# A recurrent attention and two MLPs: dummy products in one group per slot, the second MLP's weight conversion ordered behind the last attention unit

## The chip, the cores and the metric

The kernel runs on one core of one Trainium2 chip. The metric is the device time of one execution in microseconds; the kernel before takes 1383.0 us, the median of three runs (1380.85 to 1384.84).

## The reference

Three stages follow each other, all in float32 results. The first is a recurrent attention over 4 batches, 8 heads, 768 steps and a head size of 40; a 40x40 state per batch and head is read, decayed and updated at each step. Its output, 3072 tokens of 320 numbers, goes through an MLP with SiLU (320 to 2048 to 320) and then through a gated MLP (320 to 1536 twice, sigmoid gate, back to 320).

```python
for t in range(S):
    y[:, :, t] = np.einsum('bhd,bhde->bhe', rt, state)
    Sa = np.einsum('bhde,bhe->bhd', state, at)
    state = state * wt[:, :, None, :] - np.einsum('bhd,bhe->bhde', Sa, bt)
    state = state + np.einsum('bhd,bhe->bhde', vt, kt)
...
h = x @ w_in;  x = (h * sigmoid(h)) @ w_out              # first MLP
out = (sigmoid(x @ w_gate) * (x @ w_val)) @ w_out2       # second MLP
```

## The kernel before

The sequence is cut into 24 chunks of 32 steps; a chunk of one batch is a unit, so there are 96 units. One pass of the main loop (a slot) does one unit, n, on TensorE, ScalarE and VectorE in an order that is written out by hand as a string of letters: u (c_u, ps_u), R (c_rhs of the next unit, ps_r), q (c_pu, ps_lp), z and s (z_fix, ps_z, in every second slot), t (c_st, ps_t), p (prep, wt: ScalarE copies it to ks and yl), v (c_ut, ps_ut), y (c_y, ps_y: VectorE writes stg), s (c_s, ps_s, the new state). The state of unit n is wanted four units later. The digits 0 to 3 in the string are the places of the first MLP: m1_up (hp, L632) at 0 and 1, m1_down (acc, L654 to L656) at 2 and 3. The MLP lags the attention by sixteen slots, so there is none in the first sixteen; there mlp() issues dummy products instead, warm(4, 2): four products of the identity with two copies of itself (L481, acc_w), whose result nobody reads. All four products of a call go to one PSUM tile, which the next call takes anew. An opening burst of 56 such products stands ahead of the first slot.

Beside the slots run: the work on the decays of later chunks (e_work on VectorE and GpSimd, e_sys on TensorE, lb), the inversion of small triangular systems (inv_steps, on VectorE, zh and ztmp), and the conversion of the first MLP's weights. The weights come as 64-bit floats; conv_load brings a piece to a cvr tile (four of them), and conv_do makes a float32 cvt tile out of it with two ScalarE operations (L694, L695), two VectorE operations (L696, L697) and a GpSimd addition (L698). Then the piece is split into a high part (ScalarE) and a rest (VectorE).

The order of instructions on each engine is made by a scheduler with its own model of time, held by the orders that the code asks for: issue_after(x) puts what is issued in its block behind x on x's engine, without a wait between engines. in_turn() ties TensorE's work to the last product issued (last_op); behind() ties ScalarE's work behind the last unit's copy from wt (last_q["a"], L470) and VectorE's work behind the last unit's product from ps_y (last_q["v"], L575).

The second MLP's weights are converted by conv2 (L985 to L989) from the same cvr and cvt buffers, 48 pieces in all, into wgv and o tiles. Those tiles take the place of attention's in SBUF, so the last step of a piece (L988, L989) can't run before the attention is done; its first steps can. All DMAs of the kernel are issued by SP, in one queue. The second MLP then runs over 6 blocks of tokens with 12 steps of m2_up (hg, hv, L1091) and m2_down (a, L1110 to L1112).

Of the kernel before, what the change touches and what calls it, by code (L numbers as in the profile page):

```python
# [8 lines left out]
F32 = mybir.dt.float32  # L9
# [4 lines left out]
ALU = mybir.AluOpType  # L14
# [22 lines left out]
def kernel(  # L37
    ctx, tc, ins, wkab, rv, vn, w_in, w_out, w_gate, w_val, w_out2, out
):
    nc = tc.nc  # L40
# [145 lines left out]
    CW = 320  # L186
# [120 lines left out]
    def in_turn():  # L307
        return tc.issue_after(last_op[0].ins) if now[0] >= 0 else nullcontext()
# [81 lines left out]
    def behind():  # L390

        g = ExitStack()
        for x in last_q.values():
            g.enter_context(tc.issue_after(x.ins))
        return g
# [79 lines left out]
    def warm(n, w=1):  # L475

        if not n:
            return
        ps = pa.tile([128, DM], F32, tag="acc0", name="acc_w")
        for _ in range(n):  # L480
            last_op[0] = nc.tensor.matmul(  # L481
                ps[:, :128 * w], identr,
                identr.unsqueeze(1).to_broadcast([128, w, 128]), start=True, stop=True,
            )
# [139 lines left out]
    def m1_up(m, half):  # L624
        kb, p = divmod(m, NP1)
        X = X_t[kb]
        if half == 0:
            hp_t[m] = pu.tile([128, 2, 256], F32, tag="hp", name="hp")
        hp = hp_t[m]
        f = 2 * p + half  # L630
        for pi, (xi, wi_, rows) in enumerate(PASS1):
            last_op[0] = nc.tensor.matmul(  # L632
                hp[:, half, :], w1[0:rows, wi_, f * 128:(f + 1) * 128],
                X[xi][0:rows], start=(pi == 0), stop=(pi == 7),
            )
        if half == 1:
            hp_t.pop(m)
            gh = mp.tile([128, 2, 256], F32R, tag="gh", name="gh")
            gl = mp.tile([128, 2, 256], F32R, tag="gl", name="gl")

            nc.scalar.activation(hp, hp, AF.Silu, scale=wsc)  # L641
            nc.scalar.copy(gh, hp)  # L642
            nc.vector.tensor_tensor(gl, hp, gh.bitcast(F32), op=ALU.subtract)  # L643
            g_t[m] = (gh, gl)

    def m1_down(m, c):
        kb, p = divmod(m, NP1)
        gh, gl = g_t.pop(m) if c else g_t[m]
        if p == 0:
            acc_t[c] = pa.tile([128, DM], F32, tag=f"acc{c}", name=f"acc{c}")  # L650
        for fi in range(2):
            f = 2 * p + fi
            a = gh[:, fi, 128 * c:128 * c + 128]
            nc.tensor.matmul(acc_t[c], a, o1(0, f), start=(f == 0), stop=False)  # L654
            nc.tensor.matmul(acc_t[c], a, o1(1, f), start=False, stop=False)  # L655
            last_op[0] = nc.tensor.matmul(  # L656
                acc_t[c], gl[:, fi, 128 * c:128 * c + 128], o1(0, f), start=False, stop=(f == NF1 - 1)
            )
        if p == NP1 - 1:
            if c == 0:  # L660
                x2_t[kb] = mp.tile([128, 2, DM], F32, tag="cvhl", name="x2", bufs=1)
            x2 = x2_t[kb]
            nc.scalar.mul(x2[:, c], acc_t[c], wsc)  # L663
            if c:
                defer(1, lambda: nc.sync.dma_start(x2s[kb].rearrange("c p e -> p c e"), x2))
# [6 lines left out]
    def conv_load(rows, n, src, mp, cw):  # L672
        if wide:
            raw = mp.tile([128, cw, 2], I32, tag="cvr", name="cvr", bufs=4)
            t = raw.rearrange("p a b -> p (a b)")[:, :2 * n]
        else:
            raw = mp.tile([128, cw], F32, tag="cvt", name="cvt", bufs=2 + 1)
            t = raw[:, :n]
        r0 = 0
        for x in src if isinstance(src, tuple) else (src,):  # L680
            nc.sync.dma_start(t[r0:r0 + x.shape[0]], x)
            r0 += x.shape[0]
        return raw

    def conv_do(raw, rows, n, mp, cw):

        if not wide:
            return raw[:rows, :n]
        t = mp.tile([128, cw], F32, tag="cvt", name="cvt")[:rows, :n]
        lo, hi = raw[:rows, :n, 0], raw[:rows, :n, 1]  # L690
        ti = t.bitcast(I32)


        nc.scalar.mul(t, hi.bitcast(F32), 2.0 ** -112)  # L694
        nc.scalar.activation(lo, lo.bitcast(U32), AF.Copy, bias=2.0 ** 23, scale=2.0 ** -29)  # L695
        nc.vector.tensor_scalar(ti, ti, 3, None, op0=ALU.logical_shift_left)  # L696
        nc.vector.scalar_tensor_tensor(ti, hi, -0x80000000, ti, op0=ALU.bitwise_and, op1=ALU.bitwise_or)  # L697
        nc.gpsimd.tensor_tensor(ti, ti, lo, op=ALU.add)  # L698
        return t
# [85 lines left out]
    def hi_run(f, a):  # L785
        with behind(), tc.high_priority(offset=300):
            f(*a)
# [59 lines left out]
    if True:  # L847
# [12 lines left out]
        for x, t in enumerate(when):  # L860
# [7 lines left out]
            if stream[x] == e_units(gi)[-1]:  # L868
                i0 = t + 2
                i1 = min(gi * 8 - 4, i0 + 7)  # L870
                hi = lambda f: lambda *a: hi_run(f, a)
# [21 lines left out]

        def mlp(n, which):
            m = (n - 8 - 8)
            if m < 0:
                with in_turn():
                    warm(4, 2)
            if NP1 < 8 and m % 8 >= NP1:
                return  # L900
            if m < 0:
                return
            kb, p = divmod(m, 8)
            if kb >= NJ:
                return
            mm = kb * NP1 + p

            with tc.issue_after((last_op[0] if 1 else rhs_i[max(0, min(n, NS - 1) - [0, 0, 0, 0][which])]).ins):
                if which in (0, 1):
                    m1_up(mm, which)  # L910
                elif mm > 0:
                    m1_down(mm - 1, which - 2)

        for n in range(NS + 8 + 8):
# [8 lines left out]
            for o in ['cuRqz0tp1vys23l', 'zcq01uv23tpRysl'][n >= NL]:  # L923
                if o in '0123':
                    mlp(n, int(o))
# [58 lines left out]

    def conv2(tmp, src, n, hi, lo):  # L985

        w = conv_do(conv_load(128, n, src, tmp, CW), 128, n, tmp, CW)
        nc.scalar.copy(hi, w)  # L988
        nc.vector.tensor_tensor(lo, w[:lo.shape[0]], hi[:lo.shape[0]].bitcast(F32), op=ALU.subtract)  # L989

    def w2_conv(pool, tmp, x):
        f0, f1 = fc[x], min(fc[x] + 512, FF2)
        for mi in range(2):
            t = wgv[mi][x] = pool.tile([128, 6, f1 - f0], F32R, name=f"wgv{mi}_{x}")

            nc.gpsimd.memset(t[64:128, 5].bitcast(F32), 0.0)
        for o in range(f0, f1, CW2):
            n = min(CW2, f1 - o)
            c = slice(o - f0, o - f0 + n)
            for mi, w in enumerate((w_gate, w_val)):  # L1000
                t = wgv[mi][x]
                for ti in range(2):
                    conv2(tmp, wsrc(w, 128 * ti, 128, o, n), n, t[:, 2 * ti, c], t[:, 2 * ti + 1, c])

                conv2(tmp, (wsrc(w, 256, 64, o, n),) * 2, n, t[:, 4, c], t[0:64, 5, c])
# [26 lines left out]
    def o2_conv(pool, tmp, f0, f1):  # L1032
        if f1 > f0:
            t = [pool.tile([128, f1 - f0, DM], F32R, name=f"o2{y}_{f0}") for y in range(2)]
            for f in range(f0, f1):
                conv2(tmp, wsrc(w_out2, f * 128, 128, 0, DM), DM, t[0][:, f - f0], t[1][:, f - f0])
                for y in range(2):
                    o2[y].append(t[y][:, f - f0])
# [285 lines left out]
```

## Time and profile before

| | kernel before |
|---|---|
| median of three runs | 1383.0 us (1380.85 to 1384.84) |
| profiled execution, its time | 1393.2 us |
| profiled execution, its span | 1391.5 us |
| TensorE products, busy | 1320.8 us (95%) |
| VectorE busy | 798.0 us (57%) |
| ScalarE busy | 609.5 us (44%) |
| GpSimd busy | 275.5 us (20%) |
| mean granted clock of TensorE | 0.91 |

A busy TensorE is not a fast one: its clock has two levels, 1.2 GHz (shown as 0.5) and 2.4 GHz (shown as 1.0), so a stretch must be read by its busy share and its granted clock together. Times are microseconds from the start of the span. PE is TensorE, PEld its weight loads, DVE VectorE, ACT ScalarE, POOL GpSimd, SP the engine that issues the DMAs. In a timeline row a bracket gives the idle time of the engine ahead of the operation and what ended it.

### The profile page before, as it was taken

The numbers are of one execution on the slowest core, as the hardware profiler recorded it, in microseconds if no ns is written. First come the engines' busy times: TensorE is split into PE (matmuls) and PEld (weight loads), VectorE is DVE, ScalarE is ACT, GpSimd is POOL, SyncE is SP. The second block draws the span as 40 slices with busy tenths as digits, with TensorE's granted clock in tenths as the row PEclk, the third lists the DMA queues.
The fourth block names the chain that finished last, engine by engine and source line by source line (L and its number), as shares of the span: only waits on it lengthen the run. The fifth ranks groups of instructions, "written<-read, shape, count | busy, mean of one in ns | idle before, by whom it ended". The sixth has DMA issues, their size and how long they took to land. (4 is left out here: it accounts for less than half of the span.)

```text
span 1391.5 us, 43139 instructions
## 1 busy us (share of the span) xinstructions
PE 1320.8 (95%) x17921; PEld 1205.1 (87%) x17921; DVE 798.0 (57%) x2094; ACT 609.5 (44%) x1392; POOL 275.5 (20%) x357
## 2 busy tenths in 40 slices
PE   3699999996999999999999999999999999999996
PEld 3688888986999999999999999998888888888885
DVE  6345376594869687877869573367883222232321
ACT  4124443553545555455554555567652222222221
POOL 5124344441122222222121100023320000000000
PEclk9855555598899999999999999999999999999998
DMA  7655455568566667666576534134640000000000
GB/s 197 155 130 143 117 150 119 156 148 174 127 139 151 148 164 150 149 159 150 149 163 159 128 84 108 31 120 123 206 129 19 20 19 19 20 0 20 3 17 22
DMA packets 222510, 152.55 MB, mean 110 GB/s; under 512 B 131570, under 2 KB 179058, under 8 KB 222306
## 3 DMA queue, kind: packets, MB, share of 16 engines
q1 hardware_dynamic: 222306, 149.71, 43.9%
q8 instruction: 143, 2.34, 0.7%
q14 instruction: 61, 0.50, 0.1%
HBM read 106.59 MB, written 42.72 MB: 107 GB/s over the span
## 5 line engine op out<-in xcount | busy, mean ns | idle before, releaser
L632 PE MATMUL hp<-X,w 120*128 120x256 f32 x1536 | 213.2, 293 | 0.0
L632 PEld LDWEIGHTS hp<-X,w 120*128 120x128 f32 x1536 | 195.5, 196 | 3.4
L1099 DVE TENSOR_TENSOR sg<-hv,sg 128x512 f32<-128x512 f32 x72 | 49.7, 690 | 186.1 <-PE hv L1091 161.5
L1091 PE MATMUL hg<-XT,wgv 128*128 128x512 f32 x576 | 151.2, 394 | 0.5 <-ACT x L663 0.5
L1091 PE MATMUL hv<-XT,wgv 128*128 128x512 f32 x576 | 147.2, 394 | 0.0
L641 ACT ACTIVATE hp<-hp 128x512 f32<-128x512 f32 x96 | 55.9, 582 | 205.4 <-PE hp L632 205.4
L246 POOL TENSOR_TENSOR et<-et 40x256 f32<-40x256 f32 x82 | 77.2, 941 | 330.5 <-DVE ztmp L355 70.3
L654 PE MATMUL acc<-o1h,gh 128*128 128x320 f32 x384 | 126.0, 328 | 2.6 <-ACT gh L642 2.5
L1091 PEld LDWEIGHTS hv<-XT,wgv 128*128 128x128 f32 x576 | 107.3, 188 | 23.5
L1091 PEld LDWEIGHTS hg<-XT,wgv 128*128 128x128 f32 x576 | 105.9, 188 | 21.4 <-ACT x L663 0.8
L575 DVE TENSOR_TENSOR stg<-ps_y,xt 40x128 f32<-40x128 f32 x192 | 54.9, 286 | 116.1 <-PE ps_y L567 111.9
L656 PE MATMUL acc<-o1h,gl 128*128 128x320 f32 x384 | 119.8, 312 | 1.2 <-DVE gl L643 1.2
L655 PE MATMUL acc<-o1l,gh 128*128 128x320 f32 x384 | 119.1, 310 | 0.0
L643 DVE TENSOR_TENSOR gl<-hp,gh 128x512 fp32r<-128x512 f32 x96 | 65.8, 686 | 89.8 <-ACT gh L642 87.0
L698 POOL TENSOR_TENSOR cvt<-cvt,cvr 128x256 int32<-128x256 int32 (+3 forms) x85 | 73.2, 864 | 160.8 <-DVE cvt L697 65.9
L359 DVE TENSOR_TENSOR zh<-zh,ztmp 128x126 f32<-128x126 f32 (+22 forms) x310 | 98.4, 317 | 7.3
L355 DVE TENSOR_TENSOR ztmp<-zh,z 128x126 f32<-128x126 f32 (+22 forms) x310 | 98.7, 318 | 6.8 <-DMA z<-sN 1.1
L1100 ACT CAST gh<-sg 128x512 fp32r<-128x512 f32 x72 | 44.6, 620 | 124.2 <-DVE sg L1099 124.2
L1098 ACT ACTIVATE sg<-hg 128x512 f32<-128x512 f32 x72 | 42.9, 596 | 121.9 <-PE hg L1091 121.8
L481 PE MATMUL acc_w<-identr 128*128 128x256 f32 x312 | 87.7, 437 | 1.0
L1111 PE MATMUL a<-o,gh 128*128 128x320 f32 x288 | 87.9, 309 | 0.4 <-DVE o L989 0.4
L1110 PE MATMUL a<-o,gh 128*128 128x320 f32 x288 | 87.5, 310 | 0.0
(183 smaller groups left out, 2656.1 us busy)
## 6 DMA issues: line engine op xcount, KB each, us to landing
xt<-sE SPq DMA_DIRECT2D x48, 322.5 KB
sE<-et SPq DMA_DIRECT2D x84, 161.2 KB
et<-in_wkab_dram SPq DMA_DIRECT2D x40, 258.0 KB
cvr<-in_moe_w_out_dram SPq DMA_DIRECT2D x28, 320.0 KB
et<-in_wkab_dram SPq DMA_DIRECT2D x40, 193.5 KB
sZ<-z SPq DMA_DIRECT2D x44, 128.0 KB
z<-sN SPq DMA_DIRECT2D x20, 256.0 KB
cvr<-in_moe_w_in_dram SPq DMA_DIRECT2D x42, 100.0 KB
```

The source lines that it names most:

```text
L246: (nc.vector if jj == 0 and i < 1 else nc.gpsimd).tensor_tensor(av, av, wc[r, :, :, 0:C], op=ALU.mult)
L355: nc.vector.tensor_tensor(tv, z[:, 0:rows, s:s + 1].to_broadcast([128, rows, m]), nt[:, s:s + 1, s + 1:].to_broadcast([128, rows, m]), op= ...
L359: last_inv[0] = nc.vector.tensor_tensor(z[:, 0:rows, s + 1:], z[:, 0:rows, s + 1:], tv, op=ALU.add)
L481: last_op[0] = nc.tensor.matmul(ps[:, :128 * w], identr, identr.unsqueeze(1).to_broadcast([128, w, 128]), start=True, stop=True,)
L632: last_op[0] = nc.tensor.matmul(hp[:, half, :], w1[0:rows, wi_, f * 128:(f + 1) * 128], X[xi][0:rows], start=(pi == 0), stop=(pi == 7),)
L654: nc.tensor.matmul(acc_t[c], a, o1(0, f), start=(f == 0), stop=False)
L655: nc.tensor.matmul(acc_t[c], a, o1(1, f), start=False, stop=False)
L656: last_op[0] = nc.tensor.matmul(acc_t[c], gl[:, fi, 128 * c:128 * c + 128], o1(0, f), start=False, stop=(f == NF1 - 1))
L698: nc.gpsimd.tensor_tensor(ti, ti, lo, op=ALU.add)
L1091: nc.tensor.matmul(hp, wgv[mi][f // 4][0:rows, wi_, f % 4 * 128:f % 4 * 128 + 128], X[0:rows, xi, :], start=(pi == 0), stop=(pi == 7))
L1110: nc.tensor.matmul(acc2_t[t], a, o2[0][f], start=(f == 0), stop=False)
L1111: nc.tensor.matmul(acc2_t[t], a, o2[1][f], start=False, stop=False)
```

## The change

In the slots without MLP, the dummy products are issued once per slot, 24 in one call at the place 3 (behind c_s, at the slot's end), where there were four calls of four at the places 0 to 3; the calls at 2 and 3 stand next to each other, so the four calls make three pieces. And in conv2 the load of a piece is issued as before, while its conversion and split stand in a behind() block.

```diff
         def mlp(n, which):
             m = (n - 8 - 8)
-            if m < 0:
+            if m < 0 and which == 3:
                 with in_turn():
-                    warm(4, 2)
+                    warm(24, 2)
...
     def conv2(tmp, src, n, hi, lo):
 
-        w = conv_do(conv_load(128, n, src, tmp, CW), 128, n, tmp, CW)
-        nc.scalar.copy(hi, w)
-        nc.vector.tensor_tensor(lo, w[:lo.shape[0]], hi[:lo.shape[0]].bitcast(F32), op=ALU.subtract)
+        raw = conv_load(128, n, src, tmp, CW)
+        with behind():
+            w = conv_do(raw, 128, n, tmp, CW)
+            nc.scalar.copy(hi, w)
+            nc.vector.tensor_tensor(lo, w[:lo.shape[0]], hi[:lo.shape[0]].bitcast(F32), op=ALU.subtract)
```

## Rows read from the trace of the kernel before

**Rows 1.** Of the page: busy tenths in 40 slices, and TensorE's granted clock.

```profile
PE   3699999996999999999999999999999999999996
...
PEclk9855555598899999999999999999999999999998
```

**Rows 2.** Stretches: busy us (count) of PE, PEld, DVE, ACT, POOL; clock, DMA, GB/s.

```profile
70.00:105.00 35.00, 34.88 (x524) 31.18 (x524) 14.39 (x46) 9.23 (x24) 9.63 (x13) 0.50 0.53 127
...
280.00:315.00 35.00, 30.49 (x597) 28.36 (x594) 33.30 (x99) 16.65 (x43) 13.61 (x18) 0.95 0.63 153
...
420.00:490.00 70.00, 69.63 (x1390) 65.64 (x1389) 56.09 (x163) 37.32 (x88) 18.07 (x24) 1.00 0.65 149
```

**Rows 3.** Timeline of TensorE, one pair of slots: start, us, engine, line, operation.

```profile
132.00 0.76 PE L518 MATMUL ps_s<-sr,ks 128*40 128x40 f32 x16
132.69 2.50 PE L481 MATMUL acc_w<-identr 128*128 128x256 f32 x8
...
138.39 1.22 PE L481 MATMUL acc_w<-identr 128*128 128x256 f32 x4
...
157.70 0.76 PE L518 MATMUL ps_s<-sr,ks 128*40 128x40 f32 x16
```

**Rows 4.** Timeline of TensorE, the opening burst before and after the clock rose.

```profile
45.48 5.91 PE L481 MATMUL acc_w<-identr 128*128 128x256 f32 x26
...
51.19 3.67 PE L481 MATMUL acc_w<-identr 128*128 128x256 f32 x29
```

**Rows 5.** Stretches of 5 us, columns as in rows 2.

```profile
55.00:60.00 5.00, 4.50 (x116) 4.13 (x117) 0.42 (x1) 1.14 (x3) 1.17 (x3) 0.81 0.55 148
...
275.00:280.00 5.00, 5.00 (x55) 4.80 (x54) 4.87 (x16) 2.23 (x5) 2.93 (x4) 0.84 0.23 56
280.00:285.00 5.00, 4.13 (x124) 3.69 (x121) 4.76 (x15) 3.14 (x10) 2.38 (x4) 1.00 0.84 197
...
330.00:335.00 5.00, 5.00 (x68) 4.66 (x67) 0.85 (x2) 2.72 (x7) 2.65 (x4) 0.88 0.65 166
```

**Rows 6.** Timeline of TensorE, slots sixteen to twenty-three.

```profile
273.79 3.39 PE L632 MATMUL hp<-X,w 120*128 120x256 f32 x16
...
279.27 0.31 PE L656 MATMUL acc<-o1h,gl 128*128 128x320 f32 x1
...
281.21 0.48 PE L518 MATMUL ps_s<-sr,ks 128*40 128x40 f32 x16
...
283.86 0.69 PE L553 MATMUL ps_lp<-yr,vu 64*32 64x32 f32 x32 [0.77 <-DVE stg L575]
284.48 2.17 PE L632 MATMUL hp<-X,w 120*128 120x256 f32 x16
...
323.96 0.76 PE L518 MATMUL ps_s<-sr,ks 128*40 128x40 f32 x16 [4.87 <-ACT ks L469]
...
348.75 0.76 PE L518 MATMUL ps_s<-sr,ks 128*40 128x40 f32 x16 [5.62 <-ACT ks L469]
```

**Rows 7.** Timeline of ScalarE in the same slots.

```profile
321.75 0.43 ACT L694 ACTIVATE cvt<-cvr 128x256 f32<-128x256 f32 x1 [3.12 <-DMA cvr<-in_moe_w_gate_dram]
...
346.86 0.43 ACT L695 ACTIVATE cvr<-cvr 128x256 int32<-128x256 uint32 x1 [4.12 <-DMA cvr<-in_moe_w_val_dram]
```

**Rows 8.** Stretches of one pair of slots each, columns as in rows 2.

```profile
143.00:168.70 25.70, 25.59 (x376) 22.70 (x374) 9.49 (x26) 10.47 (x27) 8.55 (x11) 0.50 0.52 132
...
183.40:209.10 25.70, 25.59 (x371) 22.70 (x368) 20.48 (x56) 11.79 (x30) 13.58 (x16) 0.50 0.48 135
```

**Rows 9.** ScalarE's copies of line 988: durations in ns, first and last start.

```profile
L988 ACT CAST wgv<-cvt x36: 385/406/411, 915.2 to 1023.3; 128x256 fp32r<-128x256 f32 x36
L988 ACT CAST o<-cvt x12: 441/456/462, 942.0 to 1035.4; 128x320 fp32r<-128x320 f32 x12
```

**Rows 10.** Timeline of VectorE at the attention's end, of TensorE in the second MLP.

```profile
911.97 0.59 DVE L575 TENSOR_TENSOR stg<-ps_y,xt 40x128 f32<-40x128 f32 x2 [0.28 <-PE ps_y L567]
...
1030.36 0.42 PE L1111 MATMUL a<-o,gh 128*128 128x320 f32 x1 [0.37 <-DVE o L989]
```

## The prediction

> **What bounds the kernel now.** I read the 40 slices first. TensorE is busy nine tenths or more in nearly all of them, but in slices 3 to 8 (70 to 278 us) its granted clock is 0.5, the lower level of 1.2 GHz, against 0.8 or more in all others [rows 1]. The table of stretches says it per stage: 34.88 of 35 us busy at 0.50 from 70 us, then 0.95 from 280 us and 1.00 in the steady stage from 420 us [rows 2]. So in the first sixteen slots, before the first MLP runs, TensorE is the bound at half its clock, and much of what fills it is dummy products.
>
> Third, the timeline of TensorE in that stage. From one ps_s to the next but one (132.00 to 157.70) is a pair of slots: 25.70 us, so 12.85 us a slot [rows 3]. In each slot stand two pieces of four products at 1.22 us and two adjoining ones, shown as eight, at 2.50 us: 4.94 us. The other 12.85 - 4.94 = 7.9 us are attention. No row of the pair shows a wait: TensorE runs through.
>
> Fourth, how the clock behaves. The opening burst of 56 runs 26 products in 5.91 us (0.227 each), then 29 in 3.67 us (0.127): the upper level came at 51.2, 5.7 us after the burst began at 45.48 [rows 4]. The granted clock of 55 to 60 us is 0.81, that is 62% at 1.0, so it fell near 58.1, 3.2 us after the burst ended at 54.9 [rows 5]. It stays at 0.50 through the slots' pieces of up to 2.5 us [rows 2, 3]. It rises at about 276.6 (0.84 in 275 to 280: 68% at 1.0) [rows 5], 2.8 us into a run of hp products that began at 273.79 [rows 6].
>
> Last, the waits. After the sixteenth slot TensorE stands still twice on ScalarE's ks, 4.87 us at 323.96 and 5.62 us at 348.75 [rows 6]. In front of ks on ScalarE stand operations of the second MLP's conversion that wait for their own transfer: L694 until 321.75 (3.12 us) and L695 until 346.86 (4.12 us) [rows 7].
>
> **The change, part by part.** *Dummy products.* Removed: 16 a slot in four calls; added: 24 in one call at the slot's end, behind ps_s. At the lower clock the group costs 24 x 0.227 = 5.45 us instead of 4.94: a slot of 7.9 + 5.45 = 13.35, or +0.5 x 16 = +8 us if nothing else happened. At the upper clock it costs 24 x 0.127 = 3.05 us.
>
> The group lasts 5.45 us at the lower level, between the 2.8 us after which the clock rose in the run of hp and the 5.7 us of the opening burst; I take 4.2 us, the middle. Then 4.2 / 0.227 = 18.5 products run slowly, 5.5 quickly (0.7 us): 4.9 us, and the attention behind it starts at the upper clock. What that is worth: ps_s takes 0.76 us at the lower and 0.48 at the upper level [rows 3, 6], a ratio of 0.63; 7.9 us become 5.0.
>
> How long it lasts is bounded by two rows. After the opening burst, with the small ps_z and lb behind it, the clock fell 3.2 us later [rows 5]. Between the dense runs that end at 279.58 and begin at 284.48 stand 4.9 us of attention with 0.77 us of idle time, and the clock stays 1.00 [rows 5, 6]. If it falls 3.2 us after every group, 3.2 of the 5.0 us run quickly and the remaining 1.8 take 1.8 / 0.63 = 2.85: a slot of 4.9 + 3.2 + 2.85 = 10.95. If it holds, a slot is 5.0 + 3.05, some 8.0. The gap to be bridged is as long as that of the second row, but every second slot has ps_z, as in the first row; I take the middle, 9.5: 16 x 9.5 = 152 against 16 x 12.85 = 206.
>
> The Trainium skill, "TensorE: Matmul & The Clock Gate", section "HAM oscillation — how this bites in real kernels", describes bursts whose gaps let the clock fall, so that each burst pays the rise anew. By that rule all sixteen slots would go the first way; the gap behind the opening burst agrees (fall after 3.2 us), that at 279.58 does not (1.00 over 4.9 us) [rows 5, 6].
>
> What else lies in the stage: VectorE is busy 9.49 us in one pair, 20.48 in the fullest [rows 8]. A pair of 19 us covers all but that; against a pair at 8.0 it binds by 20.48 - 16 = 4.5 us, which I add once. In that pair ScalarE has 11.79 us and GpSimd 13.58, and a DMA share of 0.48 to 0.52 in 25.7 us becomes about 0.7 in 19: these stay covered. Nothing is queued behind the group but TensorE's own work of the next slot; ps_u and ps_r, which follow, have had the group's time for their inputs. The two pieces that go from between attention's products gave ScalarE and VectorE time: behind wt now stand only ps_ut and ps_y before ps_s needs ks. That cover is priced as a rival. Sum: 152 + 4.5 - 206 = -50 us.
>
> *Conversion.* conv_do and the two operations behind it are ordered behind the last unit's copy on ScalarE and product on VectorE; the loads are not. It is an order on the same engine, so it adds no wait of its own. Out of the slots after the sixteenth go two stalls of TensorE, 4.87 + 5.62 = 10.5 us. After the first the clock was low until 331.2 (0.88 in 330 to 335: 76% at 1.0 [rows 5]); the 7.2 us of work from 323.96 would take 0.63 of that, 2.7 less, and I take as much after the second: 5.4. At most -16. What is late next is attention's own transfers and VectorE, so I give 4 back; the ends are 0 and -16.
>
> The price is at the other end. The last unit's product is at 911.97 [rows 10] and conversion went on at 915.2 anyway [rows 9], but before that it had two tiles converted ahead, and the first steps of four more. Those operations come back; conversion advances one tile in 2.6 us (48 tiles from 915.2 to 1035.4 [rows 9]), and part of the two tiles' cost falls before 915, so some 3 us, from 0 to 7. It can be felt: TensorE waits 0.37 us for o at 1030.36 [rows 10]. GpSimd's additions and the later loads on SP's queue follow by data, when the four buffers come free; no attention transfer stands behind them by then. Sum: -16 + 4 + 3 = -9 us.
>
> Together -59 us. In the stages behind, TensorE runs through (69.63 of 70 us at 1.00 [rows 2]), so a us saved is a us off the end. The profiled execution took 1393.2 us (span 1391.5, 1.7 outside it), 10.2 more than the median 1383.0; by its own time the result is 1334, and against the median 1324. I predict 1324.
>
> **The rivals.** *The clock falls in every slot*: 16 x 10.95 + 4.5 = 180, -26 and -9: 1348. For it speaks ps_z in every second slot. The Trainium skill's rule, above, leads here. Chance 0.2.
>
> *It holds throughout and nothing else binds*: 16 x 8.0 = 128, -78 and -16: 1289. The gap at 279.58 speaks for it, the fullest pair against. Chance 0.12.
>
> *Another engine or the transfers become the bound*: were every pair as full as the fullest on VectorE plus waits, 22 us, 16 slots take 176, -30 and -9: 1344. Only one pair of eight is so. Chance 0.1.
>
> *The group is too short*, and the clock rises only as late as in the opening burst, after 5.7 us: 13.35 a slot, +8 against -9: 1382, no change. Against it speaks the rise after 2.8 us. Chance 0.07.
>
> *Slower: the lost cover.* Place: wt to ps_s, and ps_lp to ps_y, on whose evictions TensorE now waits with nothing between. VectorE makes TensorE wait 0.77 us in such a place at 283.86 [rows 6], and its queue holds the inversion's steps too. At a slot of 10.95 it decides from 2.5 us of waits a slot (12.85 + 9/16 - 10.95); with four such waits, 3.1 us, the sixteen slots give 16 x (10.95 + 3.1 - 12.85) = +19, less 9: 1393. That TensorE now waits nowhere in the pair speaks against so much. Chance 0.1.
>
> **How the numbers follow.** The forecast has 0.41, the rivals 0.2, 0.12, 0.1, 0.07 and 0.1. A difference under 0.3%, some 4 us, is what a measurement can't tell from no change. Faster: 0.41 + 0.2 + 0.12 + 0.1 = 0.83; same 0.07; slower 0.10. The range takes in the first four, 1289 to 1348, and goes on to 1370 for sizes between them and no change (half the gain of the slots and none of the conversion).
>
> **What would show it.** Slots of 9 to 10 us between one ps_s and the next; the sixteenth slot's end some 50 us earlier; a granted clock of 0.75 or more from 75 us on; acc_w as groups of 24 with a mean spacing of 0.13 to 0.2 us; no L694 of in_moe_w_gate before the last unit, and no wait of ps_s on ks over 2 us after the sixteenth slot. Wrong would be: clock 0.50 throughout with slots of 13.4 us (group too short), short slots with TensorE idle before ps_s or ps_y (lost cover), or the gain of the first stage taken back by waits for transfers between the sixteenth and twenty-fourth slot.

## The result, and the profile after

| | before | after |
|---|---|---|
| median | 1383.92 us (1380.85 to 1391.84, 4 runs) | 1340.36 us (1336.03 to 1347.32, 4 runs) |
| profiled execution, its time | 1393.2 us | 1336.0 us |
| profiled execution, its span | 1391.5 us | 1334.3 us |

The ratio is 0.968, with a 95% interval of 0.962 to 0.974: 43.6 us off by the medians, 57.2 us from profile to profile. Line numbers behind L987 are two higher in the changed kernel (L988 is L990).

First the page's slices. Against [rows 1] the run of fives in the clock is gone from slices 3 to 8, and TensorE is no longer at nine tenths in all of them:

```profile
PE   3698998899999999999999999999999999999996
...
PEclk9887888999999999999999999999999999999998
```

The stretches of [rows 2] in the changed kernel (busy us and count of PE, PEld, DVE, ACT, POOL; clock, DMA share, GB/s). The first has a clock of 0.82 instead of 0.50, and TensorE is busy for 29.84 us of 35 instead of 34.88, so it now waits 5 us in it. The steady stage is as it was.

```profile
70.00:105.00 35.00, 29.84 (x600) 27.84 (x600) 22.61 (x67) 12.92 (x35) 14.36 (x17) 0.82 0.65 159
280.00:315.00 35.00, 34.33 (x689) 32.44 (x686) 26.24 (x77) 17.05 (x41) 7.14 (x11) 1.00 0.70 165
420.00:490.00 70.00, 69.60 (x1402) 65.82 (x1398) 54.17 (x164) 36.35 (x86) 15.61 (x21) 1.00 0.67 153
```

For the sum I take stretches that begin and end with ps_s: the fifteen slots from the first ps_s to the sixteenth, once with all work and once with acc_w alone (then only PE and PEld are given). Before:

```profile
65.00:258.60 193.60, 192.74 (x2763) 171.01 (x2763) 99.93 (x289) 77.50 (x196) 74.31 (x91) 0.50 0.56 140
...
65.00:258.60 193.60, 73.29 (x240) 55.64 (x240) 0.50 0.56 140
```

After:

```profile
60.70:220.70 160.00, 145.18 (x2884) 136.77 (x2884) 114.53 (x290) 76.81 (x195) 77.98 (x92) 0.82 0.70 171
...
60.70:220.70 160.00, 63.01 (x360) 59.95 (x360) 0.82 0.70 171
```

Read by parts, a stretch is dummies + attention + idle time of TensorE. Before: 73.3 + 119.4 + 0.9 = 193.6. After: 63.0 + 82.2 + 14.8 = 160.0. So 33.6 us come from these slots. The next nine, to the twenty-fifth ps_s, took 101.1 us (258.6 to 359.7) and take 82.6 (220.7 to 303.3): 18.5 more. (They begin with the dummies of the sixteenth slot, 2.4 us before and 5.1 after.) Behind that the two kernels agree within 1 us up to the end. The remaining 4.3 us lie ahead of the first ps_s (65.0 against 60.7). Of these, 2.5 are the change's too, the dummies of the first slot at the places 0 and 1, which stood in the kernel before:

```profile
62.03 2.50 PE L481 MATMUL acc_w<-identr 128*128 128x256 f32 x8
64.47 0.61 PE L542 MATMUL ps_ut<-ident,sr 32*40 32x32 f32 x8
65.01 0.76 PE L518 MATMUL ps_s<-sr,ks 128*40 128x40 f32 x16
```

The other 1.8 us are scatter: in the kernels of this study that have no dummies there, the first ps_s comes between 57.8 and 63.9. Without them the changed kernel gained some 55 us in its profile. The kernel before was profiled in one of its slower executions: of its 34 in the jobs below, the eight with a granted clock of 0.922 or more took 1367.8 to 1380.9 us and the eight with 0.909 or less, this one among them, 1389.7 to 1394.8, so the medians (43.6 us) are the measure of the gain, and the parts read from its profile add up to more.

Where the idle 14.8 us sit is to be seen in a slot. The timeline of TensorE in the fourth (start, us, what; in brackets the idle time and what ended it):

```profile
94.01 4.02 PE L481 MATMUL acc_w<-identr 128*128 128x256 f32 x24
97.96 0.76 PE L507 MATMUL ps_u<-rb0f,zs0f 96*32 96x40 f32 x16
...
100.08 0.69 PE L553 MATMUL ps_lp<-yr,vu 64*32 64x32 f32 x32 [0.78 <-DVE z L359]
...
102.74 0.66 PE L466 MATMUL wt<-ident,xt 40*64 40x40 f32 x8 [1.57 <-ACT sr L508]
...
106.89 0.75 PE L567 MATMUL ps_y<-yr,yl 128*40 128x32 f32 x16 [2.73 <-DVE yr L556]
107.44 0.74 PE L518 MATMUL ps_s<-sr,ks 128*40 128x40 f32 x16
```

ScalarE in the same slot: sr, the eviction of the ps_u that had ended at 98.7, comes at 102.26, because in front of it the conversion's L694 waits until 101.74 for a cvt tile that GpSimd still uses.

```profile
101.74 0.49 ACT L694 ACTIVATE cvt<-cvr 128x320 f32<-128x320 f32 x1 [6.62 <-POOL w L722]
102.26 0.42 ACT L508 ACTIVATE sr<-ps_u 32x320 f32<-32x320 f32 x1
```

VectorE: yr, for which ps_y waits, stands behind the inversion's steps and runs at 106.41. The same form of step takes 0.21 us or 0.7 to 0.97.

```profile
100.10 0.77 DVE L355 TENSOR_TENSOR ztmp<-z,zh 128x60 f32<-128x60 f32 x1
100.90 0.96 DVE L359 TENSOR_TENSOR z<-z,ztmp 128x60 f32<-128x60 f32 x1
...
102.95 0.21 DVE L355 TENSOR_TENSOR ztmp<-z,zh 128x48 f32<-128x48 f32 x1
...
105.51 0.87 DVE L359 TENSOR_TENSOR z<-z,ztmp 128x15 f32<-128x15 f32 x1
106.41 0.42 DVE L556 TENSOR_TENSOR yr<-ps_lp,msk 64x256 f32<-64x256 f32 x1
```

The waits of TensorE from 60 to 260 us (total, times, longest): many small ones on VectorE and ScalarE. Of the two waits for ks of [rows 6] (10.5 us) 0.4 us are left, over the whole run too.

```profile
PE ps_y L567 <- DVE yr L556: 6.8, 4, 2.7
PE ps_u L507 <- DVE rb1r L498: 4.1, 2, 3.3
...
PE wt L466 <- ACT sr L508: 1.6, 1, 1.6
...
PE ps_s L518 <- ACT ks L469: 0.4, 1, 0.4
```

At the second MLP, the last stage of the conversion (line 990; durations in ns, first and last start) and VectorE's last product of the attention:

```profile
L990 ACT CAST wgv<-cvt x36: 387/406/413, 859.1 to 966.8; 128x256 fp32r<-128x256 f32 x36
L990 ACT CAST o<-cvt x12: 444/458/465, 886.1 to 978.3; 128x320 fp32r<-128x320 f32 x12
```

```profile
855.96 0.59 DVE L575 TENSOR_TENSOR stg<-ps_y,xt 40x128 f32<-40x128 f32 x2 [0.27 <-PE ps_y L567]
```

From that product to the first copy of line 990 it is 3.1 us, and was 3.2 [rows 9, 10]; from the first to the last copy 119.2 us, and was 120.2. The conversion tied behind the last unit costs nothing there.

### The profile page after: what moved, and what is told of

Read it like the earlier page. It is cut to its first block, busy times and chain, and to the rows that moved or that the text cites. A ratio compares the mean times of both kernels' runs of the same rounds, so it can differ in the third digit from the quotient of the medians.

```text
span 1334.3 us, 43451 instructions
## 1 busy us (share of the span) xinstructions
PE 1260.3 (94%) x18049; PEld 1158.5 (87%) x18049; DVE 809.4 (61%) x2094; ACT 608.4 (46%) x1392; POOL 277.5 (21%) x357
## 5 line engine op out<-in xcount | busy, mean ns | idle before, releaser
L632 PE MATMUL hp<-X,w 120*128 120x256 f32 x1536 | 207.6, 288 | 0.0
L632 PEld LDWEIGHTS hp<-X,w 120*128 120x128 f32 x1536 | 190.0, 191 | 3.4
L656 PE MATMUL acc<-o1h,gl 128*128 128x320 f32 x384 | 120.2, 313 | 1.3 <-DVE gl L643 1.0
L698 POOL TENSOR_TENSOR cvt<-cvt,cvr 128x256 int32<-128x256 int32 (+3 forms) x85 | 73.1, 863 | 221.8 <-DVE cvt L697 151.2
L359 DVE TENSOR_TENSOR zh<-zh,ztmp 128x126 f32<-128x126 f32 (+22 forms) x310 | 101.5, 328 | 7.4
L355 DVE TENSOR_TENSOR ztmp<-zh,z 128x126 f32<-128x126 f32 (+22 forms) x310 | 100.9, 325 | 7.7 <-DMA z<-sN 2.1
L1112 PE MATMUL a<-o,gh 128*128 128x320 f32 x288 | 87.5, 310 | 0.0
L1114 PE MATMUL a<-o,gl 128*128 128x320 f32 x288 | 78.7, 310 | 0.5 <-DVE gl L1103 0.5
```

What stands on the lines that cost most here:

```text
L355: nc.vector.tensor_tensor(tv, z[:, 0:rows, s:s + 1].to_broadcast([128, rows, m]), nt[:, s:s + 1, s + 1:].to_broadcast([128, rows, m]), op= ...
L359: last_inv[0] = nc.vector.tensor_tensor(z[:, 0:rows, s + 1:], z[:, 0:rows, s + 1:], tv, op=ALU.add)
L632: last_op[0] = nc.tensor.matmul(hp[:, half, :], w1[0:rows, wi_, f * 128:(f + 1) * 128], X[xi][0:rows], start=(pi == 0), stop=(pi == 7),)
L656: last_op[0] = nc.tensor.matmul(acc_t[c], gl[:, fi, 128 * c:128 * c + 128], o1(0, f), start=False, stop=(f == NF1 - 1))
L1112: nc.tensor.matmul(acc2_t[t], a, o2[0][f], start=(f == 0), stop=False)
L1114: nc.tensor.matmul(acc2_t[t], gl[:, 128 * t:128 * t + 128], o2[0][f], start=False, stop=(f == NF2 - 1))
```

## The experiments

All ratios are to the kernel before, run on the same chip; in brackets the 95% interval. The kernels ran in several jobs, in which the median of the kernel before was 1383.9 to 1387.2 us; each was profiled once. The table gives the parts of the fifteen slots as above, from the same two stretches of each profile, and the length of the nine slots behind them, all in us. Time in which rows of dummies and of attention overlap counts to the dummies: 6.3 us before, 2.1 after.

| kernel | median | ratio | dummies + attention + idle | clock | next nine |
|---|---|---|---|---|---|
| before | 1383.9 | 1 | 73.3 + 119.4 + 0.9 = 193.6 | 0.50 | 101.1 |
| after | 1340.4 | 0.968 [0.962, 0.974] | 63.0 + 82.2 + 14.8 = 160.0 | 0.82 | 82.6 |
| e1_group_only | 1336.7 | 0.967 [0.959, 0.975] | 56.1 + 82.9 + 23.4 = 162.4 | 0.85 | 82.4 |
| e2_tie_only | 1372.4 | 0.992 [0.988, 0.995] | 72.3 + 116.3 + 0.9 = 189.5 | 0.52 | 85.0 |
| e3_group16 | 1347.5 | 0.972 [0.967, 0.977] | 47.0 + 87.3 + 29.6 = 163.9 | 0.77 | 94.4 |
| e4_pieces_of_6 | 1352.5 | 0.976 [0.968, 0.984] | 77.0 + 89.4 + 9.6 = 176.0 | 0.76 | 87.5 |
| e5_no_dummies | 1337.3 | 0.967 [0.959, 0.974] | 0 + 125.4 + 33.0 = 158.4 | 0.50 | 81.8 |
| e6_group40 | 1356.0 | 0.978 [0.973, 0.983] | 84.3 + 81.3 + 10.1 = 175.7 | 0.89 | 87.5 |
| e7_every_second | 1339.9 | 0.967 [0.963, 0.972] | 32.5 + 97.4 + 21.7 = 151.6 | 0.70 | 91.2 |
| e8_light_conv | 1336.3 | 0.966 [0.960, 0.972] | 58.5 + 81.3 + 17.0 = 156.8 | 0.85 | 84.9 |
| e9_few_loads | 1323.3 | 0.959 [0.949, 0.969] | 0 + 125.5 + 21.9 = 147.4 | 0.50 | 83.3 |
| e10_half_inversion | 1326.7 | 0.961 [0.951, 0.971] | 0 + 125.0 + 28.5 = 153.5 | 0.50 | 82.2 |
| e11_more_at_end | 1342.9 | 0.974 [0.964, 0.984] | 35.8 + 98.8 + 21.7 = 156.3 | 0.71 | 90.9 |
| e12_spread_loads | 1353.3 | 0.982 [0.973, 0.992] | 0 + 124.7 + 23.3 = 148.0 | 0.50 | 105.8 |

**The two parts alone.** The changed kernel without the tie of the conversion:

```diff
 def conv2(tmp, src, n, hi, lo):
-        raw = conv_load(128, n, src, tmp, CW)
-        with behind():
-            w = conv_do(raw, 128, n, tmp, CW)
-            ...
+        w = conv_do(conv_load(128, n, src, tmp, CW), 128, n, tmp, CW)
+        ...
```

> The first part of the change alone: 24 dummy products in one group per slot, conversion not tied. Theory (the clock): the sixteen slots take some 10.7 us as in the changed kernel, TensorE's clock is at the upper level about two thirds of that stage; the waits of ps_s on ks of about 5 us after the sixteenth slot come back. 35 us faster than before (30 to 40), the rest of the change's gain missing. Rival (the conversion gives most of it, and the slots were shortened by it too): less than 20 us faster.

Measured: 1336.7 us, no slower than with the tie. The waits for ks, which I had expected back, did not come. And the kernel before with the tie alone:

```diff
             m = (n - 8 - 8)
-            if m < 0 and which == 3:
+            if m < 0:
                 with in_turn():
-                    warm(24, 2)
+                    warm(4, 2)
```

> The second part alone: conversion tied, four pieces of 4 dummy products as before. Theory: the sixteen slots stay at 12.85 us with the clock at 0.5, the two waits of ps_s on ks go, 8 to 18 us faster than before. Rival (transfers or VectorE are late next and take the waits' place): within 4 us of before.

Measured: 1372.4 us. The grouping alone gives 47.4 us and the tie alone 11.8, but both together no more than the grouping (43.6). The timeline of ScalarE in e1 shows it. Its conversion of the second MLP isn't tied and runs its first steps early, as before, but the transfers come sooner: against 3.12 and 4.12 us [rows 7] its waits for the gate's and the value's weights are

```profile
264.12 0.43 ACT L694 ACTIVATE cvt<-cvr 128x256 f32<-128x256 f32 x1 [0.38 <-DMA cvr<-in_moe_w_gate_dram]
...
274.31 0.43 ACT L695 ACTIVATE cvr<-cvr 128x256 int32<-128x256 uint32 x1 [1.11 <-DMA cvr<-in_moe_w_val_dram]
```

and TensorE's wait for ks, over the whole run, is the same as in the changed kernel:

```profile
PE ps_s L518 <- ACT ks L469: 0.4, 1, 0.4
```

In e2, with the old slots and the tie, the wait is 0.3 us in all. So either edit removes the stalls: the nine slots take 82.4 us with the one, 85.0 with the other, 82.6 with both. In e2 the fifteen slots keep nearly their old length, with a clock of 0.52, so the 16.1 us that its nine slots gained (101.1 to 85.0) are the tie's doing, in these two profiles; the medians give the tie 11.8 in all.

**Is it the grouping?** The same 24 products per slot, in the old places as four calls of six:

```diff
-            if m < 0 and which == 3:
+            if m < 0:
                 with in_turn():
-                    warm(24, 2)
+                    warm(6, 2)
```

> The change with the grouping undone and the number kept: 24 dummy products per slot as four calls of 6 in the old places, conversion tied. Theory (it is the grouping that lets the clock rise): clock 0.5 through the sixteen slots, each longer by 8 x 0.22 = 1.8 us than before, 14.6 us; 1395 us or more, that is 50 to 65 us slower than the changed kernel. Rival (the number of products lets it rise, wherever they stand): slots under 11.5 us, within 15 us of the changed kernel.

Measured: 1352.5 us, not the 1395 or more that I expected. The clock rose without a group of 24; in the first stretch it is even higher than with one:

```profile
70.00:105.00 35.00, 33.65 (x730) 30.02 (x727) 24.90 (x77) 14.83 (x39) 16.92 (x22) 1.00 0.67 156
```

So one group of 24 isn't needed for the clock. But e4 has groups too: its calls at the places 2 and 3 stand next to each other, as in the kernel before, and make a piece of twelve,

```profile
103.19 2.02 PE L481 MATMUL acc_w<-identr 128*128 128x256 f32 x12
```

where the kernel before has one of eight [rows 3]. Four calls of four left the clock at 0.50 (before) and 0.52 (e2), four calls of six give 0.76 over the fifteen slots, 16 in one group (e3, next) 0.77. So 16 products raise it in one group and not in pieces: their number alone doesn't decide. e4 has both a larger number and a longer piece than before, and no run tells these two apart. What the group of 24 does better is cost: 63.0 us of dummies and 82.2 of attention against 77.0 and 89.4 in the fifteen slots.

**How many?** 16 and 40 products in the group, and 24 in every second slot only.

```diff
-                    warm(24, 2)
+                    warm(16, 2)
```

> The changed kernel with 16 products in the group, as many per slot as before. Theory (what the clock gives back is what the group costs): the group takes some 3 us instead of 4.3, the clock is at the upper level for a smaller part of the stage, slots stay near 10.7 us; within 10 us of the changed kernel. Rival (the clock is what counts): the clock rises in fewer slots, slots of 11.5 us or more, over 12 us slower than the changed kernel.

```diff
-                    warm(24, 2)
+                    warm(40, 2)
```

> The changed kernel with 40 products in the group. Theory: the clock holds through most slots (0.9 or more of the stage), attention falls to some 6 us a slot with the waits for ScalarE and VectorE that are there now, the group takes 5.1 to 6; slots of 11.5 us, 10 to 20 us slower than the changed kernel. Rival (attention at the lower clock is the dear part): 5 us or more faster than the changed kernel.

```diff
-            if m < 0 and which == 3:
+            if m < 0 and which == 3 and n % 2 == 1:
```

> The changed kernel with the group of 24 in every second slot only. Theory: 8 groups of 4.3 us go, and the clock is down in half of the stage; some of it is lost to attention at the lower clock: within 10 us of the changed kernel. Rival (TensorE's own work bounds a pair: 4.3 + 6 + 8 = 18.3 us against 21.3): 20 us or more faster.

Measured: 1347.5, 1356.0 and 1339.9 us, each as the theory said. With 40 the clock is at 0.89 and attention costs hardly less than with 24 (81.3 against 82.2), but the dummies 21 us more. With 24 in every second slot the fifteen slots are 8.4 us shorter than in the changed kernel, and the nine behind them 8.6 us longer: TensorE's idle time there is 12.7 us against 6.4, and the clock falls twice (once in the changed kernel).

**None at all.** The group of 24 is gone; the opening burst stays.

```diff
-                    warm(24, 2)
+                    warm(0, 2)
```

> The changed kernel with no dummy products in the sixteen slots (the opening burst of 56 stays). Theory (dummy products are paid for by the clock that they lift): attention's own products take 7.9 us at the lower clock, other engines and chains that were hidden come up; slots of 9.5 to 11 us, so within 15 us of the changed kernel, either way. Rival (the dummies cost more than the clock gives back): slots of 8 to 9 us, 25 to 40 us faster than the changed kernel. Second rival (the clock stays low beyond the sixteenth slot and every engine waits longer): slower than the changed kernel by more than 15 us.

Measured: 1337.3 us, as fast as the changed kernel, with the clock at 0.50 in all fifteen slots:

```profile
62.40:220.80 158.40, 125.38 (x2523) 115.63 (x2524) 109.07 (x290) 76.74 (x196) 78.31 (x93) 0.50 0.68 172
```

This is the run that decides what the change is worth. Against e5 the changed kernel pays 63.0 us for dummies; the raised clock gives 125.4 - 82.2 = 43.2 of it back in attention, and 33.0 - 14.8 = 18.2 us of the dummies lie in time in which TensorE waits anyway. 63.0 - 43.2 - 18.2 = +1.6, the difference of the two stretches. With the overlap counted to attention, its rows take 125.7 us before, 125.4 in e5 and 84.2 after, so by this count the clock gives 41.2 us back. The old dummies gave no clock at all: against e5 they hid 32.1 us of waits, and the fifteen slots were 35.2 us longer with them (193.6 against 158.4).

**What are TensorE's waits?** Three kernels each lighten one suspect. In the changed kernel, the conversion of the first MLP's weights cut to its first ScalarE operation (L695 to L698 left out, so what the first MLP gets isn't its weights):

```diff
-                w = conv_do(raw_t.pop(k - 3), rows, n, mp, CW)
+                w = conv_lite(raw_t.pop(k - 3), rows, n, mp, CW)
```

> The changed kernel with four of the five steps of conv_do left out for the first MLP's weights (L695 to L698), so that ScalarE, VectorE and GpSimd have less to do in the sixteen slots; the values that the first MLP gets are not its weights. Theory (the waits in the slots that are left are for conversion's place in the queues of ScalarE and VectorE): the long slots, 12 to 14 us now, fall to 10 or less, the mean of the sixteen to 9.5, 15 to 20 us faster than the changed kernel. Rival (the inversion's steps or the transfers make them): less than 6 us faster.

Measured: 1336.3 us, the rival's case (4.1 us faster). VectorE's work in the fifteen slots falls from 114.5 to 83.6 us and GpSimd's from 78.0 to 50.7, TensorE's idle time rises by 2 us. VectorE now waits more for transfers (60 to 260 us; the row is 5.8 us in the changed kernel):

```profile
DVE wcl L229 <- DMA et<-in_wkab_dram: 20.9, 5, 9.4
```

In e5, only four loads for the first MLP instead of 79:

```diff
+            if k < 4:
+                raw4[k] = conv_load(128, DM, wsrc(w_out, 128 * k, 128, 0, DM), mp, CW)
-            raw_t[k] = conv_load(rows, n, src, mp, CW)
+            raw_t[k] = raw4[k % 4]
```

> The kernel without the 24 dummies per slot (e5_no_dummies) with, in addition, only four loads of weights for the first MLP: their data are used for all 79 pieces, so the first MLP's weights aren't its own; its products and conversions all run. In e5 TensorE is at the low clock for sixteen slots, busy 125 of 158 us from the first to the sixteenth ps_s, and the end of slot 24 is at 302.6 us, as it is in four other kernels with different dummies (299 to 305). Theory that the transfers, or SyncE which issues them, set that end: 75 loads of 40 to 320 KB, about a fifth of what the DMA moves there, go away, the 33 us in which TensorE waits shrink by half or more, the end of slot 24 comes at about 285 us and the total at about 1315. Theory that the recurrence with VectorE's inversion sets it: end of slot 24 at 298 to 306 us, total 1330 to 1340. Theory that the small waits of TensorE for evictions on VectorE and ScalarE are the whole of it, each added to TensorE's own time: also 298 to 306, since these loads stand in no such wait; between the last two e10_half_inversion decides.

And in e5, every second step of the inversion left out:

```diff
-        for s in range(s0, s1):
+        for s in range(s0, s1, 1 if gi == 0 else 2):
```

> The kernel without the 24 dummies per slot (e5_no_dummies) with, in addition, every second step of VectorE's inversion left out (two operations each) for all groups but the first, so the inverses aren't the inverses. In e5 the two lines of the inversion keep VectorE busy for 47 us between 60 and 260 us (139 us in all), and GpSimd's work lengthens them. Theory that VectorE sets the end of the slots before the first MLP, by the inversion or by the evictions that wait behind it: about 23 us less work of VectorE, end of slot 24 at 283 to 292 us instead of 302.6, total 1315 to 1325. Theory that transfers set it: no more than 5 us, total 1330 to 1340.

Measured: 1323.3 and 1326.7 us against 1337.3. The loads' absence takes 11.1 us of the 33.0 idle ones; the waits of ps_u for a state copied from ps_z (zs0f, zs1f), two of the rows in which it shows, fall from 8.5 to 1.6 us in the fifteen slots. In e5:

```profile
PE ps_u L507 <- ACT zs1f L445: 5.5, 3, 4.5
...
PE ps_u L507 <- ACT zs0f L445: 3.0, 2, 2.0
```

In e9:

```profile
PE ps_u L507 <- ACT zs1f L445: 1.1, 3, 0.5
PE ps_u L507 <- ACT zs0f L445: 0.5, 1, 0.5
```

The inversion's half takes 4.5 us of idle time (109.1 to 97.9 us of VectorE). Neither theory of a single bound holds. Nor was there a floor at 299 to 305 us for the end of the nine slots, the twenty-fifth ps_s: it came there in five kernels (after, e1, e5, e7, e8), but at 318 to 328 in e3, e4 and e6, which I had left out of that count, and at 293.0 in e9 and 297.3 in e10. The waits are a sum of several causes; these loads are the largest that was found, and if the two effects add up, which no run shows, a good half of the 33 us (33.0 - 11.1 - 4.5 = 17.4) has no cause that these runs single out.

**Two tries for a better kernel.** Groups in every second slot, and in each of the last three:

```diff
-            if m < 0 and which == 3:
+            if m < 0 and which == 3 and (n % 2 == 1 or n > 13):
```

> The changed kernel with the group of 24 in every second slot up to the twelfth (as in e7_every_second, which had the shortest stage of all, 151.6 us from the first to the sixteenth ps_s, but lost 9 us against the changed kernel in slots 16 to 24, with the clock down twice there) and then in each slot of the last three. Theory that the dummies in front of slot 17 keep the clock up there and nothing else is due: stage 153 us, slots 16 to 24 82 us, total 1327 to 1332, some 8 us better than the changed kernel. Rival: work other than TensorE's sets the end of slot 24 at 299 to 305 us in whatever way the dummies are placed, then what the earlier slots gain is given back in slots 15 to 20, total 1334 to 1341.

Measured: 1342.9 us: the rival, and a little more. The nine slots take 90.9 us, as long as in e7. And e5 with the first MLP's loads and conversion spread over 24 slots:

```diff
-                need = w_ * (n + 1) // (8 + 8 + 3)
+                need = w_ * (n + 1) // 24
```

> The kernel without the 24 dummies per slot (e5_no_dummies, 1337 us, end of slot 24 at 302.6 us) with the loads and conversions of the first MLP's weights spread over 24 slots instead of 19; nothing of the computation is left out. With all but four of these loads gone (e9_few_loads) the stage from the first to the sixteenth ps_s took 147.4 us instead of 158.4, and the end of slot 24 came 9.6 us earlier. Theory that what counts is how many loads and conversions stand in the first sixteen slots: a fifth of them moves behind, the stage takes 154 to 156 us, slots 16 to 24 stay at 82, total 1332 to 1335, under both kernels. Rival: the pieces that move come into the slots where the products of the first MLP need them, ScalarE and GpSimd are late there, TensorE waits for a weight and may lose the clock once, slots 16 to 24 take 86 us or more, total 1337 to 1345.

Measured: 1353.3 us: the rival again, and more of it. The fifteen slots gain 10.4 us, more than I gave them, and the nine lose 24.0. TensorE's waits there, from the sixteenth to the twenty-fifth ps_s:

```profile
PE ps_u L507 <- DVE rb1r L498: 10.9, 3, 5.9
PE hp L632 <- DMA w<-lo: 8.7, 1, 8.7
```

A product of the first MLP waits 8.7 us for its weight, and the clock falls behind it (0.50 from 297 to 307 us). No kernel of the study beats the changed one by more than the runs scatter with the whole computation done; e1 and e5 are level with it and simpler.

## Why the prediction was right, and where not

**The sum.** It gave 1334 us for the profiled execution, against 1336.0 measured, and 1324 for the median, against 1340.4. The step from the one to the other failed: I took the whole sum off the median of three runs, though the profiled execution of before lay 10 us above it. The profiles differ by 57.2 us, the medians by 43.6: the profiled execution of before lay 9.3 us above its median and that of after 4.3 below. On record the time of the kernel before falls as its granted clock rises (1394.8 us at 0.902, 1367.8 at 0.932), and it was profiled at 0.909. So the sum was taken from an execution with little of the upper clock, and others have less to gain; in which stage they have more of it no run shows, since only one was profiled. That the profile's sum came out within 2 us is in part luck, as the terms show.

**What bounds the kernel.** Right: TensorE at half its clock, with dummies filling it. But I priced the dummies only as a means for the clock. That they might go without a price was no case of mine, and e5 shows that they can.

**The slot's 9.5 us of TensorE.** Right as a size: (63.0 + 82.2) / 15 = 9.68. The way there was half right. Groups last 3.1 to 5.3 us, 4.2 on average (63.0 / 15), where I took 4.9; attention takes 82.2 / 15 = 5.5, where 9.5 leaves it 4.6. That the two errors cancel is luck. The clock fell ten times in the fifteen slots, so in two slots of three. That is near the condition of the rival that gave 1348; its price was wrong, since the clock stayed up for longer than the 3.2 us that I took from the opening burst [rows 5]. In the fourth slot it held for 4.9 us behind the group, with waits in between, and later for 5.7 us. The Trainium skill's rule of bursts that each pay the rise anew ("TensorE: Matmul & The Clock Gate", section "HAM oscillation — how this bites in real kernels") agrees with the trace in part: ten rises in the fifteen slots and a clock of 0.82, but in the other five the clock held from one group to the next.

**Other engines: 4.5 us.** This is the term that was mis-sized: TensorE waits for 14.8 us, and a slot took 10.67 us. I had asked only whether an engine's busy time fits into a pair of slots, and only the fullest pair did not. VectorE is busy for 114.5 of 160 us and no bound by that count; in the slot shown what costs time is the order in its queue and in ScalarE's, where evictions stand behind inversion steps and conversions. How much of the 14.8 us is of this kind is not shown: with the conversion lightened (e8) they did not shrink, and half of the inversion was worth 4.5 us, in e5. TensorE idle before ps_y (6.8 us) was one of the signs of being wrong that I had named. It is the mechanism of the rival "lost cover", at 1.0 us a slot instead of the 2.5 from which it would have decided. Of the fifteen slots I expected 15 x (9.5 - 12.85) + 4.5 = -45.7 and got -33.6: 10.3 of the missing 12.1 us are this term, 2.7 are 9.68 against 9.5, and -0.9 is before's slot, 12.91 against 12.85.

**Conversion: -16 + 4 + 3.** The nine slots gave 18.5 us, the worst that came late in them was a wait of 3.3 us for rb1r at 256 us, and the end cost nothing. So the term was too small by 9.5 us, and this covered most of what the other missed, by luck. But it isn't the tie's term: e1 gets all of it without the tie. I added two edits as if each had its own stall to remove, and they shared one. Why the shorter slots remove it is shown only in part: in the kernel before the first load of the gate's weights was issued at 315.46 us and kept ScalarE waiting until 321.75, with a DMA share of 0.98 in between; in e1 it was issued at 261.21 and the wait ended at 264.12, with a share of 0.73. That the load met fewer other transfers there fits this, and no run tests it.

**The signs I had named.** Slots of 9 to 10 us: 10.67. The sixteenth slot's end some 50 us earlier: 38 (258.6 and 220.7 at its ps_s). Clock 0.75 or more from 75 us: 0.82. Groups spaced by 0.13 to 0.2 us: 4.2 / 24 = 0.175 on average. No L694 of the gate's weights before the last unit: the first runs at 851.4 us, behind the last unit's copy. No wait for ks over 2 us: 0.4.

## What to carry to other kernels

Dummy products that raise the clock are to be weighed against none at all, not only against other dummies: here the whole account (63 us paid, 43 back from the clock, 18 hidden in waits) came out even, and a kernel without them was as fast. When two edits remove waits of the same chain, price them together, because the first to land takes the gain. And once the bound engine is sped up, read the order in the queues of the engines that feed it: busy time far under the slot's length doesn't keep an eviction from standing behind something slow.

## What the hardware showed that I had not expected

The clock fell while TensorE ran through. From 123 to 137 us of the changed kernel it was busy for 14.00 of 14 us at the upper level, with a group of 24 from 128.17 to 131.31, and from 137.0, with no idle time, it had 0.50 (stretches, columns as above):

```profile
96.00:103.00 7.00, 4.65 (x94) 4.25 (x94) 6.74 (x16) 1.21 (x3) 6.14 (x7) 0.99 0.60 156
103.00:113.00 10.00, 7.12 (x69) 6.73 (x68) 6.85 (x20) 5.23 (x14) 4.14 (x7) 0.50 0.59 113
123.00:137.00 14.00, 14.00 (x346) 13.22 (x346) 8.89 (x19) 8.48 (x21) 8.31 (x10) 0.99 0.66 176
137.00:140.40 3.40, 3.40 (x43) 3.28 (x39) 2.89 (x6) 2.22 (x7) 3.25 (x5) 0.50 0.36 63
```

From 96 to 103 us it held with TensorE busy for 4.65 us of 7. So idle time is not what made it fall at 137.0: what ran there, for 5.7 us behind the group, were attention's own small products. In e5, with these products alone, it stayed at 0.50 over all fifteen slots.

VectorE's work grew with the change. The fifteen slots have the same 290 instructions (289 before), and they take 114.5 us instead of 99.9. It isn't only that they are pressed into less time: e6 has 115.2 us in 175.7, e9 110.8 in 147.4. The inversion's products (L355, zh) went from a mean of 336 to 452 ns with the same shapes and count, though the median stayed (264 and 268 ns): a few became very long, the longest 2122 ns instead of 916.

```profile
L355 DVE TENSOR_TENSOR ztmp<-zh,z 128x126 f32<-128x126 f32 (+22 forms) x31 | 14.0, 452 | 0.5
```

In the slot shown above the long ones at 100.10 and 100.90 stand beside GpSimd's sums,

```profile
99.88 0.90 POOL L721 TENSOR_TENSOR lo<-cvt,w 56x320 fp32r<-56x320 f32 x1
100.86 0.85 POOL L722 TENSOR_TENSOR w<-cvt,w 40x320 fp32r<-40x320 f32 x1
```

and end 0.09 and 0.15 us behind them (100.87 and 100.78, 101.86 and 101.71). That at 105.51 stands beside another (105.47 to 106.34), and the short one at 102.95 in a gap of GpSimd's work (102.6 to 103.25). Three short steps, at 97.14, 97.51 and 99.85, have GpSimd beside them. Over the fifteen slots of the changed kernel all 22 of the 92 inversion steps (L355, L359) that took 0.5 us or more ran beside GpSimd for at least four fifths of their time (14 such steps before), and the 47 steps with no GpSimd beside them took 0.16 to 0.30 us. The Trainium skill ("GPSIMD Engine Reference", section "1. Specifications") says that GpSimd shares its SBUF interfaces with VectorE, with contention for instructions of VectorE that read two SBUF operands, as these do; the rows agree with that. No run here took GpSimd's work away to show it by itself, since e8 lightened VectorE and GpSimd together.
